# One written list of all steps in place of due times for a list scheduler, in a gated linear attention and gated MLP kernel

## The chip, the cores and the metric

The kernel runs on one core of a Trainium2 chip. The metric is the time of one execution in microseconds (us), measured on the device.

## The reference, cut to what matters

Two parts follow each other: a linear attention with a gated state, and an MLP whose gate mixes the tokens of one batch. There are 4 batches of 768 tokens, 8 heads of 48 features, so 384 features per token.

```
f = 1 / (1 + exp(-f_logit))
for t in range(S):                                   # attention, per batch and head
    state = f[t, :, None] * state + outer(k[t], v[t])
    x[t] = q[t] @ state
h = gelu(x @ w_in)                                   # 384 -> 1024
u, v = h[..., :512], h[..., 512:]
v_n = (v - mean(v)) / sqrt(var(v) + 1e-6) * g_ln
gated = u * (w_sg @ v_n + b_sg)                      # w_sg: 768 x 768 over tokens
out = x + gated @ w_out                              # 512 -> 384
```

`w_in` and `w_out` come as 64-bit words and are converted on the chip.

## The kernel before, in words

The 3072 tokens are 24 tiles of 128, numbered n = 0 to 23, six to a batch; three tiles make a group g = 0 to 7. All work is cut into 1551 named steps: 1533 that the function body adds with `plan.add`, and 18 fillers. A step is nearly always one instruction off TensorE, and a run of matmuls on it. The names that matter here, with the lines that the profile shows:

- Loads on SyncE's queue: `f`, `k`, `q`, `v` of a tile, `cs` (constants: an identity, a triangle, a mask; L1028), `ldin` and `ldout` (two blocks of columns of a weight; L505), `ldsg`, `out`.
- The gate: `e`, `l` (exponential and logarithm on ACT, L435), `cum` (sum over time on TensorE, L632), `up`, `dn` (exponentials on ACT, L435), `mq`, `mk` (q and k times them, L654 and L649).
- The attention of a tile: `tr`, `do` (transposes and decay on TensorE in the first batch, L684 and L669; later batches turn through DRAM instead), `tc`, `di` (copies out, L440), `su` (scores and state update, 64-wide matmuls, L729 and L734), `ms` (mask, L739), `sa`, `sm` (state, L755 and L758), `w` (copy of v, L440), `y` (result, 64-wide matmuls, L777), `ty`, `jy`.
- The MLP: `xT`, `xh`, `xl` (transpose x and split it into two float32r parts), `hv`, `hu` (v and u halves), `gv`, `gu` (GELU on ACT), `ns`, `nd`, `nq`, `nr`, `nh`, `nl` (normalization; `nl` is L867), `sg` (mix over tokens), `sb`, `sm_`, `sh`, `sl` (gate and split), `po` (output matmul), `re` (residual). All large matmuls stand on L801.
- Weights: `wa`, `wp`, `wq`, `wr`, `wc`, `wd`, `we`, `wf` convert a block on ACT, DVE or POOL (L514 to L552); `wT`, `wh`, `wl` do `w_sg`.

Each matmul group takes one of four PSUM buffers (`ps_b`) and gives it back when its reader is done. ACT holds one table at a time: `e`, `l`, `up`, `dn` need one, `gv`, `gu` the other, and each change is an ACT_TABLE_LOAD (L433).

What sets the order: `Plan.run` is a list scheduler with a small model of engine times. `dues` gives each step a due time from its users, `MOVES`, a table of numbers found by search, shifts these and fixes some engines, and the scheduler takes on each engine the ready step with the earliest due time. The result is sorted by the planned start, and each engine's program is that sequence. `Plan.warm` then puts fillers (matmuls of zeros, L1179) on TensorE wherever the plan leaves it idle in the first 45 us: as many columns of 128 as fit the gap by the model. Fillers are real instructions: TensorE runs them whether the gap is there on the chip or not.

Of the kernel before, what the change touches and what calls it, by code (L numbers as in the profile page):

```python
# [71 lines left out]
wpin4:-0.300 wqin4:14.900 wcin4:-0.750 wein4:-3.400:ACT wfin4:21.900 ldin5:7.200 wain5:36.600 wpin5:0.300 wqin5:44.500
wcin5:-0.400 wdin5:17.300 wein5:69.700 ldin6:-164.800 wain6:-41.350 wqin6:23.000 wrin6:24.100 wdin6:-2.500
wein6:-1.400:ACT wfin6:0.000:DVE ldin7:-57.800 wpin7:-0.500 wqin7:-0.100 wrin7:22.500 wdin7:-4.200:DVE wein7:0.600
wfin7:0.000:DVE ldout0:731.600 waout0:-2.000 wqout0:25.950 wrout0:3.950 wcout0:2.100 wdout0:2.900:DVE
weout0:-149.400:ACT wfout0:69.600:POOL ldout1:-12.800 waout1:27.200 wpout1:3.300 wrout1:-7.900 wcout1:-215.200
# [5 lines left out]
f0:-380.900 k0:-176.300 q0:-163.100 v0:-109.900 w0.0:-8.300:DVE w0.1:14.100:ACT cum0:-19.800 up0:-0.800 mq0:4.600
mk0:33.900 do0:1.600 di0:99.700:ACT tc0.0:-101.000:DVE tc0.1:-60.200:ACT ms0:-3.600 sm0.1:-57.100:DVE ty0:0.700
jy0:2.050 xh0:5.000 hv0:17.700 gv0:-3.450 ns0:-11.900 nd0:25.400 nh0:-21.150 nl0:-15.900 re0:-999999918.050
out0:-999999960.000 f1:-357.200 v1:5.350 w1.0:45.900:ACT w1.1:18.500:POOL e1:0.400 l1:32.100 cum1:93.100 up1:100.600
mq1:117.000:POOL mk1:0.000:DVE do1:-20.000 di1:-42.500:ACT tc1.0:48.000:ACT tc1.1:26.300 su1:-7.500 sm1.0:0.800:POOL
sm1.1:61.500 xT1:30.900 xh1:-4.800 xl1:-53.100 hv1:0.600 gv1:6.200 nh1:-6.900 nl1:-126.700 out1:-999999857.100
f2:-115.700 k2:-1.100 q2:16.400 v2:54.000 w2.0:42.300:ACT w2.1:16.000 e2:-65.600 cum2:15.400 up2:-1.400 mq2:0.000:DVE
di2:51.200 tr2:44.700 tc2.0:-0.000:ACT tc2.1:-3.000 su2:-5.700 ms2:26.000 sa2.0:-0.100 sm2.0:-2.100:DVE
sm2.1:58.000:POOL y2:-247.400 ty2:9.450 xT2:0.500 xl2:25.900 ns2:2.400 nd2:42.700 nr2:61.600 nh2:9.000:ACT nl2:11.150  # L90
hu0.0:1148.900 gu0.0:0.800 sb0.0:5.400 sm_0.0:-0.200 sh0.0:-75.200:ACT hu0.1:523.900 gu0.1:77.900 sg0.1:68.000
sb0.1:-21.000 sm_0.1:0.000:DVE hu0.2:51.700 gu0.2:24.200 sg0.2:6.900 sb0.2:-1.350 sm_0.2:15.200:POOL sh0.2:-0.300:ACT
sl0.2:-1.550 hu0.3:-2.300 gu0.3:39.100 sg0.3:5.500 sb0.3:-3.500 sm_0.3:0.000:POOL sh0.3:-230.100:ACT sl0.3:-71.700
po2:17.000 re2:67.300 f3:-2.900 k3:104.100 q3:76.900 v3:55.300 w3.0:0.000:ACT w3.1:18.100:DVE e3:-9.100 l3:-43.700
cum3:-120.000 up3:43.600 dn3:0.100 mq3:2.350:DVE do3:-15.300 di3:-9.200:ACT tr3:22.100 tc3.0:-37.900:ACT
tc3.1:-7.450:ACT su3:138.000 ms3:-197.500 sm3.0:-0.700:DVE sa3.1:-20.250 sm3.1:-0.700 jy3:-1.700 xT3:337.100
xl3:49.600 hv3:14.400 ns3:33.900 nd3:61.000 nq3:25.500 nr3:-15.800 nh3:-7.850 nl3:32.300 po3:6.450 f4:-4.300 q4:26.350
v4:53.000 w4.0:20.150 w4.1:-2.900 e4:40.900 up4:-37.500 dn4:20.000 mq4:1.600:DVE di4:-22.300 tc4.0:0.000:DVE
tc4.1:4.400:DVE ms4:5.900 sa4.0:-20.550 sm4.0:0.000:POOL sm4.1:-20.600:DVE ty4:0.100 jy4:39.150 xT4:27.200 xl4:-0.500
hv4:18.000 ns4:7.500 nq4:37.800 nr4:0.500 nh4:19.400:ACT nl4:53.200 out4:-16.400 f5:-143.700 k5:27.900 q5:33.000  # L100
w5.0:-0.600:DVE w5.1:1.400:POOL e5:157.100 l5:-0.100 cum5:-3.900 dn5:-83.200 mq5:3.700 mk5:1.200:DVE do5:0.900
tc5.0:-9.200 tc5.1:0.500:ACT su5:35.900 sm5.0:-58.600 y5:-65.300 ty5:39.550 jy5:1.400 xl5:7.900 ns5:-27.500
nd5:-44.400:ACT nq5:2.000 nr5:-10.400 nh5:0.000:ACT hu1.0:8.950 gu1.0:-0.050 sg1.0:-54.300 sb1.0:-0.800
sm_1.0:-13.900:POOL sh1.0:121.300 sl1.0:-1.500 hu1.1:-30.500 sg1.1:691.400 sb1.1:0.100 sm_1.1:58.400 sh1.1:15.600:DVE
hu1.2:21.500 sg1.2:-167.000 sm_1.2:8.900:DVE sh1.2:-10.100 sl1.2:-56.500 hu1.3:-34.350 gu1.3:89.000 sm_1.3:7.750:DVE
sl1.3:-0.100 po5:-15.150 re5:-999999877.700 k6:-1.100 v6:1.200 w6.0:-9.400:DVE e6:-2.300 l6:-16.700 lh6:-45.700:DVE
ll6:-23.850:POOL cum6:1679.100 up6:45.550 dn6:-89.650 mq6:-1.900:DVE mk6:-49.900:DVE do6:44.000 tt6.1:2.200
to6:-16.300 ti6.0:50.200 ti6.1:50.000 tc6.0:123.500 tc6.1:13.600:DVE su6:27.700 sz6:-41.350 sa6.0:0.400 sm6.0:-0.800
sa6.1:-0.900 sm6.1:71.700:POOL y6:-3.400 jy6:1.400 xT6:-1.900 xh6:5.300 xl6:-28.900 gv6:-0.500 ns6:2.600 nd6:14.600
nr6:-47.100 nh6:214.400 po6:64.900 out6:-999999809.250 f7:-29.800 k7:6.600 q7:-2.400 v7:-1.100 w7.1:0.000:ACT  # L110
l7:-1.700 lh7:0.000:DVE ll7:-13.500:DVE up7:-1.300 dn7:116.100 mq7:-5.100 mk7:0.000:POOL di7.0:-12.700 tt7.0:12.700
tt7.1:-183.200 ti7.0:22.900 ti7.1:100.050 ti7.2:-0.250 ti7.3:-0.600 tc7.0:108.200:ACT tc7.1:-4.850:DVE sm7.0:0.200
sa7.1:999999923.500 sm7.1:999999864.600 ty7:-0.200 jy7:75.400 xT7:23.000 xh7:-6.800 gv7:119.500 ns7:0.100
nd7:22.200:ACT nr7:3.050 nl7:-3.400 f8:6.000 k8:-51.900 w8.0:-120.600 w8.1:157.900:ACT e8:5.300 l8:-40.200 lh8:-64.200
ll8:-9.100:POOL up8:6.800 mq8:10.800 do8:-34.300 di8.1:9.500 tt8.1:-8.700 ti8.0:-13.300 ti8.1:81.600 ti8.2:153.400
tc8.0:17.300:DVE tc8.1:-10.600:ACT su8:-8.400 ms8:-20.200 sa8.0:999999908.000 sm8.0:59.900:POOL sa8.1:999999905.650
sm8.1:139.700:POOL y8:9.400 ty8:-5.400 xT8:-4.400 xh8:-75.100 xl8:6.600 hv8:-7.800 gv8:0.950 ns8:-129.550 nd8:0.200
nq8:-12.800 nh8:-0.200 nl8:-23.900 gu2.0:2.450 sg2.0:8.000 sb2.0:17.600 sm_2.0:4.700:DVE sh2.0:-78.600 hu2.1:-14.450
sb2.1:5.450 sm_2.1:22.100 sh2.1:71.000 hu2.2:1.000 gu2.2:1.300 sg2.2:11.700 sm_2.2:5.400:POOL sh2.2:0.000:ACT
sl2.2:-18.900 hu2.3:-1.600 gu2.3:-1.800 sg2.3:-2.650 sb2.3:5.400 sm_2.3:0.000:DVE sh2.3:20.100:ACT po8:9.400 re8:4.700  # L120
out8:-999999780.000 f9:0.700 k9:10.600 w9.0:999999899.600 w9.1:-19.400:ACT l9:-30.300 lh9:-10.700:DVE ll9:15.450:POOL
cum9:-472.700 dn9:15.400 mq9:-84.000 mk9:5.500 di9.0:130.900 di9.1:72.600 tt9.0:103.700 ti9.0:-51.200 ti9.1:103.800
ti9.2:-3.500 ti9.3:-30.500 tc9.0:204.500 tc9.1:-12.600 sa9.0:-93.150 sm9.0:-0.400 sa9.1:26.550 sm9.1:64.100 jy9:-0.600
xh9:35.550 xl9:37.200 hv9:-3.100 gv9:153.600 ns9:-11.150 nd9:-4.100:DVE nq9:85.300 nr9:3.000 nh9:0.000:ACT nl9:14.100
po9:22.700 f10:-29.100 q10:0.400 v10:35.200 w10.0:27.600:DVE w10.1:-16.100:POOL e10:94.000 l10:-17.300 lh10:17.600:ACT
# [1173 lines left out]
```

## Time and profile before

| | us |
|---|---|
| median of 3 runs | 364.99 (364.79 to 365.52) |
| the profiled execution, its own time | 364.8 |
| its span, first to last instruction | 363.0 |
| TensorE busy, fillers with it | 355.3 |
| VectorE (DVE) busy | 252.1 |
| ScalarE (ACT) busy | 224.4 |
| GpSimd (POOL) busy | 64.9 |

1.8 us of the execution lie outside the span. The granted clock of TensorE is 1.00 of full speed in all slices of the span. TensorE's busy time counts overlapping matmuls once and takes in the fillers, so it is not all useful work; the idle time of its weight loads (PEld) shows small waits that the busy time hides.

### The profile page before, as it was taken

The page shows a single profiled execution, that of the slowest core. Times are in us where ns is not written, and L with a number is a line of the kernel's source. Part 1 is how long each engine was busy: PE and PEld are TensorE (multiplying, and loading weights), DVE is VectorE, ACT ScalarE, POOL GpSimd, SP SyncE. Part 2 cuts the span into 40 slices and gives each one's busy share as a digit, 9 for nine tenths or more (in the row PEclk, how much of TensorE's full clock was granted, in tenths as well). Part 3 has the DMA queues.
Part 4 walks back from the last instruction along what each step waited for, and adds up shares of the span by engine and source line. Part 5 has one row for each costly group of instructions (what it writes and reads, how often), then busy time and mean ns, then how long its engine had stood idle before and what let it go on. Part 6 is the DMA issues. An engine that isn't in the chain of part 4 may idle for free.

```text
span 363.0 us, 11355 instructions
## 1 busy us (share of the span) xinstructions
PE 355.3 (98%) x4672; PEld 324.1 (89%) x4672; DVE 252.1 (69%) x586; ACT 224.4 (62%) x476; POOL 64.9 (18%) x113
## 2 busy tenths in 40 slices
...
GB/s 195 225 230 198 226 158 251 91 54 161 164 182 205 203 179 223 151 2 117 129 192 135 162 162 118 23 24 109 88 154 70 243 67 2 3 22 2 0 44 94
DMA packets 134047, 45.90 MB, mean 126 GB/s; under 512 B 117221, under 2 KB 130405, under 8 KB 133990
## 3 DMA queue, kind: packets, MB, share of 16 engines
...
## 4 chain that ended last, share of the span: by engine, by line
PE 94%; DMA 3%; ACT 1%; SPq 1%; DVE 0%; issue 0%
PE ps_b L801 69%; PE ps_y L777 7%; PE ps_s L729 4%; PE ps_b L1179 3%; PE ps_b L806 2%; PE ps_s L734 2%; PE ps_b L684 2%; DMA vs<-in_v_dram 1%; PE ps_b L669 1%; DMA cs<-in_consts_dram 1%; PE ps_b L632 1%; PE ps_b L635 1%; PE ps_b L561 1%; PE ps_b L636 1%; PE ps_b L1034 0%; ACT L433 0%
## 5 line engine op out<-in xcount | busy, mean ns | idle before, releaser
L801 PE MATMUL ps_b<-w_sg_hi,vh 128*128 128x384 f32 x192 | 65.5, 341 | 0.0
L801 PE MATMUL ps_b<-w_sg_hi,vh_lo 128*128 128x384 f32 x192 | 64.9, 338 | 0.0
L801 PE MATMUL ps_b<-w_sg_lo,vh 128*128 128x384 f32 x192 | 64.8, 338 | 0.0
L801 PE MATMUL ps_b<-w_out_hi,gg 128*128 128x384 f32 x174 | 48.3, 339 | 0.0
L433 ACT ACT_TABLE_LOAD x29 | 37.2, 1283 | 0.5
L801 PEld LDWEIGHTS ps_b<-w_sg_hi,vh 128*128 128x128 f32 x192 | 36.0, 188 | 0.3
L801 PEld LDWEIGHTS ps_b<-w_sg_lo,vh 128*128 128x128 f32 x192 | 36.1, 188 | 0.0
L801 PEld LDWEIGHTS ps_b<-w_sg_hi,vh_lo 128*128 128x128 f32 x192 | 36.0, 188 | 0.0
L801 PEld LDWEIGHTS ps_b<-w_out_hi,gg 128*128 128x128 f32 x174 | 31.8, 188 | 0.2
L777 PEld LDWEIGHTS ps_y<-vs,st 64*64 64x64 f32 x768 | 24.4, 134 | 5.4 <-issue 3.5
L801 PE MATMUL ps_b<-w_out_lo,gg 128*128 128x384 f32 x87 | 29.1, 335 | 0.0
L801 PE MATMUL ps_b<-xTh,w_in_hi 128*128 128x384 f32 x84 | 29.1, 346 | 0.0
L894 DVE SCALAR_TENSOR_TENSOR tmp<-ps_b,cols,b_bc 128x384 f32<-128x384 f32 x32 | 19.5, 608 | 13.7 <-PE ps_b L801 13.7
L801 PE MATMUL ps_b<-xTl,w_in_hi 128*128 128x384 f32 x84 | 28.4, 338 | 0.0
L801 PE MATMUL ps_b<-xTh,w_in_lo 128*128 128x384 f32 x84 | 28.4, 338 | 0.0
L435 ACT ACTIVATE f<-f 128x384 f32<-128x384 f32 x48 | 25.1, 526 | 4.4 <-DMA f<-in_f_logit_dram 4.0
L777 PE MATMUL ps_y<-vs,st 64*64 64x48 f32 x768 | 27.2, 220 | 0.0
L777 PE MATMUL ps_y<-S,sk 48*64 48x48 f32 x768 | 27.0, 220 | 0.0
L435 ACT ACTIVATE u<-ps_b 128x384 f32<-128x384 f32 x32 | 15.4, 490 | 17.5 <-PE ps_b L801 17.4
L801 PE MATMUL ps_b<-w_in_hi,xTh 128*128 128x512 f32 x63 | 25.6, 406 | 0.4 <-ACT u L435 0.4
L801 PE MATMUL ps_b<-w_in_hi,xTl 128*128 128x512 f32 x63 | 24.9, 395 | 0.0
L801 PE MATMUL ps_b<-w_in_lo,xTh 128*128 128x512 f32 x63 | 24.8, 394 | 0.0
...
## 6 DMA issues: line engine op xcount, KB each, us to landing
...
```

Of the source, the lines that this page charges most:

```text
L433: nc.scalar.preload_act_table_set(SETS[want])
L435: nc.scalar.activation(dst, src, func, **kw)
L561: nc.tensor.transpose(ps[:, j], t[:, (hf * KT + j) * P : (hf * KT + j + 1) * P], ident)
L632: nc.tensor.matmul(ps, tril, f_raw[n], start=True, stop=True)
L684: nc.tensor.transpose(psum[f"tr{n}"][j][:W2, p * P : (p + 1) * P], kq[:, j, 2 * p : 2 * p + 2, :].rearrange("t h d -> t (h d)")[:, :W2], i ...
L729: nc.tensor.matmul(ps_s[rows(score_rows(c, 2 * p + par)), par, p * C : (p + 1) * C], sk[r, 0, p, c], sk[r, 1, p, c], start=True, stop=True)
L734: nc.tensor.matmul(ps_s[feat(par), c, 256 + p * D : 256 + (p + 1) * D], kt[rows(c), h], vs[rows(c), h], start=True, stop=True)
L777: nc.tensor.matmul(ps_y[rows(c), half, h * D : (h + 1) * D], a, m, start=start, stop=stop)
L801: nc.tensor.matmul(ps, a, m, start=(j == 0), stop=(j == len(seq) - 1))
L806: nc.tensor.transpose(ps[:, j], x_sb[n][:, j * P : (j + 1) * P], ident)
L894: nc.vector.scalar_tensor_tensor(t, psum[f"sg{g}.{ft}"][:, :E], g_col[:, ft : ft + 1], b_bc[:, tokens(g)], op0=ALU.mult, op1=ALU.add)
L1179: steps = plan.warm(plan.run(), 45.0, lambda k, n: nc.tensor.matmul(ps_b[k][:, : n * P], zeros, zeros[:, None, :].to_broadcast((P, n, P)), ...
```

## The change

`MOVES`, `dues` and the scheduler's choice go. In their place stands `ORDER`, one list of all 1533 steps, each with its engine where that isn't the step's first choice. `run` walks the list once: each step starts when its engine, its needs, its buffers and its bank are free by the same model, and the steps are again sorted by that start. The functions that issue instructions, the needs, the buffers and `warm` are as before.

```
-MOVES = """
-cs:-176.800 cum_c:-122.400 g:-72.700 b:-1.500 bb0:-18.050 bc0:-65.600:DVE bc1:-30.500 zy:-149.600 zs:1.500
...
+ORDER = """
+clear f0 cs ldin1 k0 ldin4 wain1 e0 l0 f1 q0 f2 ldin6 v0 ldin7 q1 k1 v1 ldin0 k2 f3 cum0 wpin1 wqin1 wrin1 up0 dn0
+wain4 wcin1 wdin1 zs zy wein1 e1 l1 wfin1 wpin4 wqin4 mk0:POOL mq0 tr0 cum1 do0 wain6 tc0.0 tc0.1 up1 di0:ACT dn1
...
     def run(self):
-        self.dues()
-        for name, us, *e in (x.split(":") for x in MOVES.split()):
-            s = self.by[name]
-            s["due"] += float(us)
-            if e:
-                s["engines"] = {e[0]: s["engines"][e[0]]}
...
+        for item in ORDER.split():
+            name, *e = item.split(":")
+            s = self.by[name]
+            e = e[0] if e else next(iter(s["engines"]))
+            s["engines"] = {e: s["engines"][e]}
+            t = max([s["after"], free[e]] + [self.by[x]["end"] + self.SEM for x in s["needs"]])
+            s["got"] = []
             for r in s["take"]:
...
+                at, i = min(self.rings[r])
+                self.rings[r].remove((at, i))
+                s["got"].append(i)
+                t = max(t, at)
```

What the program becomes, in numbers of instructions and steps:

| | before | after |
|---|---|---|
| matmuls other than fillers | the same | the same |
| columns of filler ahead of `cum0` | 1664 | 1920 |
| columns of filler from `cum0` to `y0` | 3072 | 3840 |
| columns of filler after `y0` | 2816 | 896 |
| ACT_TABLE_LOADs of L433 | 29 | 21 |
| the same up to the first `gu` | 5 | 3 |
| steps on ACT, DVE, POOL | 374, 559, 79 | 375, 524, 113 |
| DVE steps ahead of `ns1` (mean of tile 1) | 75 | 62 |
| turns between 64-wide steps (`su`, `y`) and others on TensorE | 58 | 56 |

Of the 13 steps that leave DVE ahead of `ns1`, the balance by kind is `wd` -3, `wf` -3, `w` -3, `mk` -2, `wc`, `wl`, `tc` and `sm` -1 each, `we` +2.

TensorE at the start. The program before, from the first filler to the first `su`; L632 is `cum`, L684 `tr`, L669 `do`:

```order
L1179 MATMUL ps_b_67<-zeros 128x512 x3
L1179 MATMUL ps_b_67<-zeros 128x128
L632 MATMUL ps_b_67<-f,cs 128x384
L632 MATMUL ps_b_68<-f,cs 128x384
L1179 MATMUL ps_b_69<-zeros 128x512
L1179 MATMUL ps_b_67<-zeros 128x512
L1179 MATMUL ps_b_67<-zeros 128x384
L684 MATMUL ps_b_69<-cs,kq_90 112x128 x4
L684 MATMUL ps_b_70<-cs,kq_90 112x128 x4
L669 MATMUL ps_b_67<-cs,eb_102 112x2 x4
```

And now, the same place (L1031 is the filler, L484 `cum`, L536 `tr`, L521 `do`):

```order
L1031 MATMUL ps_b_67<-zeros 128x512 x3
L1031 MATMUL ps_b_67<-zeros 128x384
L484 MATMUL ps_b_67<-f,cs 128x384
L1031 MATMUL ps_b_68<-zeros 128x512 x2
L1031 MATMUL ps_b_67<-zeros 128x512 x3
L1031 MATMUL ps_b_67<-zeros 128x256
L536 MATMUL ps_b_68<-cs,kq_90 112x128 x4
L536 MATMUL ps_b_69<-cs,kq_90 112x128 x4
L484 MATMUL ps_b_70<-f,cs 128x384
L521 MATMUL ps_b_67<-cs,eb_102 112x2 x4
```

Between `cum0` and `tr0` stand 2816 columns of filler where `cum1` and 1408 columns stood; `cum1` comes after `tr0`.

ACT at the start, before; L435 with `flag_e` is `e`, the next `l`, then `up` (`eb`) and `dn`; L514 is `wa`, L440 CAST `we`:

```order
L415 ACT_TABLE_LOAD
L435 ACTIVATE f,flag_e<-f 128x384
L435 ACTIVATE f<-f 128x384
L435 ACTIVATE f,flag_e<-f 128x384
L435 ACTIVATE f<-f 128x384
L514 ACTIVATE u<-gg 128x384
L435 ACTIVATE eb_102<-ps_b_67 128x8x48
L435 ACTIVATE f<-ps_b_67 128x384
```

And now (L287 for L435, L366 for L514):

```order
L267 ACT_TABLE_LOAD
L366 ACTIVATE u<-gg 128x384
L287 ACTIVATE f,flag_e<-f 128x384
L287 ACTIVATE f<-f 128x384
L287 ACTIVATE eb_102<-ps_b_67 128x8x48
L287 ACTIVATE f<-ps_b_67 128x384
L366 ACTIVATE u<-gg 128x384
L292 CAST w_in_hi_75<-u 128x3x128
```

The first `wa` moves ahead of `e0` and `l0`, and `e1`, `l1` move behind `dn0`. On SyncE's queue the loads begin `f0`, `cs`, `ldin1`, `k0`, `ldin4`, `f1`, `q0` where they began `f0`, `f1`, `ldin1`, `cs`, `k0`, `ldin4`, `q0`.

POOL at the start, before, behind the memsets of `clear`; L654 is `mq`, L440 `w`, L758 `sm`, L855 and L856 `nr`:

```order
L1037 MEMSET raw 1x128
L654 ISA
L654 TENSOR_TENSOR kq_91<-kq_91,eb_103 128x8x48
L440 COPY vs_94<-vs_94 64x192
L758 TENSOR_TENSOR S_101<-S_101,dec 112x192
L758 TENSOR_TENSOR S_100<-S_100,dec 112x192
L758 TENSOR_TENSOR S_101<-S_101,dec 112x192
L855 TENSOR_SCALAR vg_rs<-vg_mv 128x1
```

And now (L501 is `mk`, L506 `mq`, L610 `sm`, L388 `wd`, L404 `wf`):

```order
L333 MEMSET cols 128x1
L501 ISA
L501 TENSOR_TENSOR kq_90<-kq_90,f 128x8x48
L506 TENSOR_TENSOR kq_91<-kq_91,eb_103 128x8x48
L966 MEMSET S_100 112x192
L610 TENSOR_TENSOR S_101<-S_101,dec 112x192
L388 TENSOR_TENSOR u<-u 128x384
L610 TENSOR_TENSOR S_101<-S_101,dec 112x192
L404 TENSOR_TENSOR w_in_lo_78<-u,w_in_hi_76 128x3x128 x2
```

`mk0`, `wdin7`, `wfin7` and `wfin5` have come to POOL from DVE, and `mk0` is now its first TENSOR_TENSOR.

## Rows read from the trace of the kernel before

**Rows 1.** The page: busy time of each engine, and the chain of work that ended last by engine.

```profile
PE 355.3 (98%) x4672; PEld 324.1 (89%) x4672; DVE 252.1 (69%) x586; ACT 224.4 (62%) x476; POOL 64.9 (18%) x113
...
PE 94%; DMA 3%; ACT 1%; SPq 1%; DVE 0%; issue 0%
```

**Rows 2.** Busy time of each engine by stretches of the span (us from its start; after the stretch its length, then the engines in the order PE, PEld, DVE, ACT, POOL, TensorE's granted clock, the DMA engines' share, GB/s).

```profile
0.00:20.00 20.00, 17.15 (x186) 10.95 (x187) 13.32 (x33) 12.82 (x31) 2.85 (x14) 1.00 1.03 215
20.00:40.00 20.00, 19.97 (x337) 14.44 (x336) 18.91 (x49) 16.45 (x39) 2.10 (x4) 1.00 0.98 221
40.00:55.00 15.00, 15.00 (x364) 12.24 (x364) 13.13 (x36) 14.71 (x31) 4.80 (x9) 1.00 0.86 174
55.00:70.00 15.00, 14.59 (x146) 12.65 (x139) 11.61 (x30) 14.63 (x36) 3.20 (x6) 1.00 0.66 172
70.00:100.00 30.00, 30.00 (x236) 29.22 (x236) 25.45 (x53) 23.52 (x52) 9.79 (x12) 1.00 0.53 129
```

**Rows 3.** All waits of PE over the span (who, for whom, us in total, times, longest).

```profile
PE ps_b L632 <- DMA cs<-in_consts_dram: 1.8, 1, 1.8
PE ps_b L1179 <- DVE zeros L1181: 1.0, 1, 1.0
PE ps_b L801 <- ACT u L435: 0.4, 1, 0.4
```

**Rows 4.** Waits of the weight loads (PEld) in the first 75 us; the same columns.

```profile
PEld ps_b L801 <- ACT u L435: 0.7, 1, 0.7
PEld ps_b L806 <- ACT sk L440: 0.6, 1, 0.6
```

**Rows 5.** Waits of the weight loads from 75 us to the end, the two longest in total.

```profile
PEld ps_y L777 <- issue: 3.2, 11, 0.4
PEld ps_s L729 <- issue: 1.0, 4, 0.3
```

**Rows 6.** The timeline of the first 16 us, some of its rows: start, us, engine, line, and in brackets the idle time before it and what ended that. L435 `f<-f` is `e` and then `l`, L514 `wa`, L1029 a copy that waits for `cs` alone, L632 `cum`, L1179 the filler, L684 `tr`.

```profile
1.05 4.54 PE L1179 MATMUL ps_b<-zeros 128*128 128x512 f32 x8 [1.05 <-DVE zeros L1181]
...
3.74 0.52 ACT L435 ACTIVATE f<-f 128x384 f32<-128x384 f32 x1 [1.73 <-DMA f<-in_f_logit_dram]
...
4.39 0.52 ACT L435 ACTIVATE f<-f 128x384 f32<-128x384 f32 x1
...
5.19 0.52 ACT L435 ACTIVATE f<-f 128x384 f32<-128x384 f32 x1 [0.28 <-DMA f<-in_f_logit_dram]
...
6.68 0.55 ACT L514 ACTIVATE u<-gg 128x384 f32<-128x384 f32 x1 [0.31 <-DMA gg<-in_moe_w_in_dram]
...
7.28 0.23 DVE L1029 CAST cum<-cs 128x128 fp32r<-128x128 f32 x1 [5.03 <-DMA cs<-in_consts_dram]
...
7.39 1.53 PE L632 MATMUL ps_b<-f,cs 128*128 128x384 f32 x4 [1.80 <-DMA cs<-in_consts_dram]
...
8.76 2.52 PE L1179 MATMUL ps_b<-zeros 128*128 128x512 f32 x6
...
11.12 1.04 PE L684 MATMUL ps_b<-cs,kq 128*112 128x128 f32 x8
```

**Rows 7.** The timeline of TensorE from 18 to 27 us: the first row of `y0`, the filler behind `su1` and the first row of `y1`.

```profile
18.24 0.26 PE L777 MATMUL ps_y<-vs,st 64*64 64x48 f32 x2
...
23.70 2.84 PE L1179 MATMUL ps_b<-zeros 128*128 128x512 f32 x6
26.48 0.26 PE L777 MATMUL ps_y<-vs,st 64*64 64x48 f32 x2
```

**Rows 8.** DVE's groups of the first 40 us: count, busy us, mean ns of one, idle before. L536 is `wd`, L552 `wf`, L649 `mk`, L440 `vs` is `w`, L531 `wc`, L527 (`wr`) the shortest 128x384 operation.

```profile
L531 DVE SCALAR_TENSOR_TENSOR u<-gg,u 128x384 f32<-128x384 uint32 x7 | 4.1, 580 | 0.1
...
L536 DVE TENSOR_TENSOR u<-u 128x384 f32<-128x384 f32 x7 | 3.8, 548 | 0.0
L552 DVE TENSOR_TENSOR w_in_lo<-u,w_in_hi 128x384 fp32r<-128x384 f32 x6 | 3.2, 552 | 0.0
L649 DVE TENSOR_TENSOR kq<-kq,f 128x384 f32<-128x384 f32 x5 | 2.8, 550 | 0.3 <-DMA kq<-in_k_dram 0.3
...
L527 DVE TENSOR_SCALAR u<-u 128x384 uint32<-128x384 uint32 x7 | 2.5, 354 | 0.1
...
L440 DVE COPY vs<-vs 64x192 f32<-64x192 f32 x5 | 1.3, 255 | 0.1
```

**Rows 9.** The page's group of ACT table loads.

```profile
L433 ACT ACT_TABLE_LOAD x29 | 37.2, 1283 | 0.5
```

**Rows 10.** POOL's timeline up to 17 us: its last memset of the start and its first TENSOR_TENSOR.

```profile
2.17 0.20 POOL L1037 MEMSET raw<- 1x128 f32 x1
15.85 1.02 POOL L654 TENSOR_TENSOR kq<-kq,eb 128x384 f32<-128x384 f32 x1 [13.48 <-ACT u L514]
```

**Rows 11.** One DVE line over the span (`nl`): duration in ns min/median/max, first and last start in us.

```profile
L867 DVE SCALAR_TENSOR_TENSOR vh_lo<-vg,vg_rs,vh x24: 707/752/1447, 43.9 to 317.4; 128x512 fp32r<-128x512 f32 x24
```

**Rows 12.** POOL's timeline around 136.5 us, one row.

```profile
136.46 1.01 POOL L649 TENSOR_TENSOR kq<-kq,f 128x384 f32<-128x384 f32 x1 [2.03 <-DVE vg_mv L840]
```

**Rows 13.** DVE's timeline at the same place, the `nl` beside it.

```profile
136.57 1.45 DVE L867 SCALAR_TENSOR_TENSOR vh_lo<-vg,vg_rs,vh 128x512 fp32r<-128x512 f32 x1
```

**Rows 14.** The end: the last residual on DVE.

```profile
358.56 0.56 DVE L925 TENSOR_TENSOR tmp<-ps_b,x 128x384 f32<-128x384 f32 x1 [1.56 <-PE ps_b L801]
```

More of the change, by code (lines that the diff above doesn't have):

```diff
@@ L72 @@
[L72 to L76, printed above, removed]
@@ L82 @@
[L82 to L86, printed above, removed]
@@ L87 @@
[L87 to L125, printed above, removed]
-ll10:84.950 cum10:-17.600 dn10:-12.500 mq10:-6.600:POOL mk10:999999972.750 do10:65.900 di10.0:35.750 di10.1:0.650
```

271 lines of the change are left out of this document (87 added, 184 removed).

## The prediction

> **What bounds the kernel now.** I read the page first, then the stretches, then the waits, then the timeline of the start. TensorE is busy for 355.3 us of the 363.0 us span and carries 94% of the chain that ended last [rows 1]. Over the whole span it waits three times: 1.8 us for `cs`, 1.0 us for the zeros of its own filler, 0.4 us for a GELU [rows 3]. From 75 us on its weight loads show only short waits, most of them "issue" at the 64-wide steps, 0.4 us at most [rows 5]. So nothing done behind the first 75 us can give much: the matmuls are the same in both programs, and there they follow each other without a gap. What is left is the start, where the busy time deceives: it holds 5888 columns of filler behind `cum0`. Those stand where TensorE has nothing to do, because the engines that feed it are late: DVE is busy 18.91 of 20 us from 20 to 40 us, ACT 14.71 of 15 from 40 to 55 and 14.63 of 15 from 55 to 70, while POOL has 2.10 of 20 [rows 2]. The granted clock is 1.00 throughout [rows 2], so a filler column costs the same before and after.
>
> **The change part by part.**
>
> *The first loads and ACT's first steps.* Loads land in the order of the queue. By the first users, `f0` was there at 3.74, `f1` at 5.19, `ldin1` at 6.68, `cs` at 7.28 [rows 6]: steps of 1.45, 1.49 and 0.60 us. `cum0` began at 7.39, 0.11 behind `cs`. Now the queue is `f0`, `cs`, `ldin1`: `cs` at 3.74 + 0.60 = 4.34, `ldin1` at 5.83. So `cs` no longer holds `cum0`; but ACT does the first `wa` ahead of `e0`, so `e0` waits for a weight that it doesn't need. `wa` takes 0.55, `e0` to `l0` 4.39 - 3.74 = 0.65, `l0` 0.52 [rows 6]: 5.83 + 0.55 + 0.65 + 0.52 = 7.55, and with the 0.11 `cum0` begins at 7.66, **0.3 later** than it did. Bounds: 0, if the loads come 0.3 sooner than the steps say; +1.1, if `ldin1` lands no sooner than it did. I take 0.3, the value of the rows themselves. The first filler block ran from 1.05 for 4.54 [rows 6]; 256 columns more, 0.4 by the next paragraph, end it at 6.0, and it is no term.
>
> *Fillers.* Behind `cum0`, 1408 columns ran from 8.76 to the start of `tr0` at 11.12 [rows 6]: 2.36 us, 1.676 ns a column. From `cum0` to `y0` there are now 768 more, +1.3 us; behind `y0` 1920 fewer, -3.2 us. Together 1152 fewer: **-1.9 us**. `y0` itself, at 18.24 before [rows 7], so comes late, at about 18.24 + 0.3 + 1.3 = 19.8, and the gain is made behind it.
>
> *What must hold for that.* TensorE is given its 3.2 us back only if the others feed it sooner after `y0`. For this speaks the work taken from DVE. By the balance of the 13 steps ahead of `ns1`, at 548 ns for `wd`, 552 for `wf`, 550 for `mk`, 580 for `wc`, 255 for `w` [rows 8], -3, -3, -2, -1, -3 make 1.64 + 1.66 + 1.10 + 0.58 + 0.77 = 5.7 us; two `we` come back, which this trace doesn't show on DVE (354 ns is the nearest, the shortest operation of that size [rows 8]): -0.7; `wl`, `tc` and `sm`, one each, are left out as small. So about **5 us of DVE's work** leave a stretch in which it is full, for 3.2 us less filler. On ACT two of five table loads go ahead of the first `gu`, at 1283 ns [rows 9] 2.6 us, in the stretch where it is full. The six table loads that go later are worth nothing: there TensorE waits for nobody [rows 5]. The same holds for the 34 steps that POOL takes over in all, as far as they stand later.
>
> *Old waits.* In 55 to 70 us the weight loads wait 0.7 for a GELU and 0.6 for a copy by ACT [rows 4]; of PE's own time 0.4 is lost [rows 3]. With two table loads fewer ahead of it I take **-0.4** (0 to -1.0).
>
> *Turns.* There are 56 turns between 64-wide and other steps, not 58. No row prices a turn alone; the "issue" waits ahead of 64-wide steps, 3.2 us in 11 [rows 5], are the nearest, 0.3 each and hidden in part: **-0.1** (0 to -0.6).
>
> *New waits.* Fillers absorb lateness; with few left behind `y0`, a late step of ACT, DVE or POOL is now a wait of TensorE. Nearest are the old waits at the places without filler, 0.4 to 0.7 each [rows 3, 4]. One of them: **+0.5** (0 to +3.2, all that was cut there).
>
> *The end* is the same: `po23`, its residual at 358.56 [rows 14], the store. The last gate product goes to POOL, 1.01 [rows 12] for some 0.55, and two output matmul groups stand between it and its reader; no term, and 0.5 if they were not there.
>
> The sum: +0.3 - 1.9 - 0.4 - 0.1 + 0.5 = **-1.6 us**. Against the profiled execution's own 364.8 that gives 363.2; the median of the runs is 0.2 above that execution, so the median after should be **363.4**.
>
> **The rivals.**
>
> *Deeper (chance 0.14).* DVE's 5 us and ACT's 2.6 us are more than the plan spends, so no new wait comes and the old ones go whole: +0.3 - 1.9 - 1.0 - 0.1 = -2.7, a median of 362.3. For it speaks that the filler ahead of `y1`, 2.84 us long [rows 7], stood there while DVE was full; against it, that fillers are run even where the gap is gone, so relief beyond them is worth only the waits.
>
> *POOL holds DVE (0.17).* Where a POOL operation of 1.01 us began at 136.46, an `nl` that began at 136.57 took 1.45 us [rows 12, 13]; the median is 752 ns [rows 11]. So it lost 0.69. Ahead of `su5` POOL now has 14 such steps, not 8. Six times 0.69 is 4.1 us, most of the 5 us that DVE was spared; then three or four waits of 0.4 to 0.7 stand behind `y0`, some 2 us in place of 0.5: 364.9, no change. Against it: only the few that meet lose that much, as the median shows. The Trainium skill has the rule in "SBUF — State Buffer", section "Who interferes with whom": a DVE instruction with two SBUF inputs and a GpSimd one that reads SBUF share a port that one of them holds whole. By that rule a DVE operation that begins just behind a POOL one would lose nearly its whole 1.01, so six of them 6 us as an estimate, and the cut of filler would come back as waits, about 365 too; the trace agrees that the one stands while the other runs, and shows that most don't meet.
>
> *The dense stretch isn't fed (0.11), slower.* Place: TensorE from `y0` to the first `hu`. `su1` now comes straight behind `y0`, and `tr1` ahead of it, so the chains `su`, `sa`, `sm`, `ms`, `y` and `cum`, `up`, `mq`, `tr` must close within about one other step each, on a DVE queue where weight steps stand between. If they take as long as they did, the 3.2 us of filler come back whole as waits, while the 1.3 us ahead of `y0` and the 0.3 of `cum0` stay: +1.5 with the turns, a median of 366.5. It decides from 2.1 us of waits in that stretch, where the sum without new waits (+0.3 - 1.9 - 0.4 - 0.1) is used up. Against it stand the 5 us of DVE's work.
>
> *POOL isn't ready (0.03), slower.* Ahead of its first TENSOR_TENSOR the program has an ISA instruction of POOL; its cost is not in the rows, since 13.48 us of idle time lay over it [rows 10]. Now that first one is `mk0`, which `tr0` needs by about 7.66 + 0.7 + 4.7 = 13.1 (one `cum`, then the filler [rows 6]), so at 1.02 us [rows 10] it must begin by 12.1, 9.7 us behind the memsets. If it needed the whole 13.48 it would begin at 15.9: 3.8 us late, and a median of 367.2. The Trainium skill, "GPSIMD Engine Reference", section "Instruction dispatch", gives about 6 us for the first call of freshly loaded code: by that, ready at 8.4 as an estimate, and no delay. No run here shows it.
>
> **How the numbers follow.** The forecast, 362.8 to 364.2, has 0.55; with the deeper case 0.69 for faster. The case of POOL holding DVE lies within 0.2%, about what a measurement of this kernel can tell from no change (364.3 to 365.7): 0.17. The slower two: 0.14. For the range I go down to the deeper case, 362.2, and up to 365.4, which takes in the larger part of the middle case and leaves out the slower ones and a little at either end, 0.2 in all.
>
> **What would show it.** Right: `cum0` at 7.5 to 7.9; `tr0` at 13 to 13.4 straight behind its filler, not behind a wait; `y0` at 19.5 to 20.2; few PE or weight-load waits between 20 and 55 us; the last residual at 357, not 358.6; DVE below 18 of 20 us from 20 to 40. Wrong: `tr0` released by `mk0` or `mq0` behind the end of its filler (POOL or DVE late at the start); waits of 2.1 us or more between `y0` and the first `hu` (not fed); DVE operations there of twice their median beside POOL's (held); or a wait of TensorE behind 75 us, which would mean that the later order, which I took to be free, costs something.

## The result, and the profile after

| | before | after |
|---|---|---|
| median, us | 365.01 (364.61 to 366.75, 9 executions) | 367.2 (365.98 to 369.7, 9 executions) |
| ratio, 95% interval | | 1.0052 (1.0028 to 1.0076) |
| the profiled execution, its span | 364.8, 363.0 | 369.7, 367.5 |

The kernel became slower by half a per cent; 363.4 had been forecast, with a range up to 365.4. The profiled execution of after is the longest of its nine, so its sizes are near the upper end; a second one is in the first experiment.

The page of after, against [rows 1]:

```profile
PE 356.5 (97%) x4672; PEld 326.4 (89%) x4672; DVE 246.5 (67%) x551; ACT 211.6 (58%) x469; POOL 93.6 (25%) x147
...
PE 76%; DMA 8%; DVE 6%; ACT 4%; SPq 3%; issue 2%; POOL 0%; ACTq 0%; DVEq 0%
```

TensorE's share of the chain fell from 94% to 76%, and DMA, DVE and SyncE's queue are in it: a first sign that TensorE is no longer fed without a gap. The stretches, columns as in [rows 2]:

```profile
0.00:20.00 20.00, 17.76 (x120) 10.17 (x120) 12.34 (x26) 11.75 (x27) 4.74 (x15) 1.00 1.07 215
20.00:40.00 20.00, 19.57 (x400) 16.21 (x399) 17.78 (x40) 15.72 (x38) 6.39 (x8) 0.91 1.04 214
40.00:55.00 15.00, 15.00 (x366) 12.71 (x365) 13.09 (x35) 13.61 (x33) 4.49 (x9) 1.00 0.48 119
...
70.00:100.00 30.00, 29.70 (x234) 29.11 (x233) 25.41 (x52) 22.59 (x48) 11.90 (x13) 1.00 0.68 153
```

DVE is relieved (17.78 of 20 us from 20 to 40, forecast below 18), but not by the 5 us of work that the prediction counted: ahead of `ns1` its busy time is 30.0 us in place of 31.2, with 13 steps fewer. New against this profile of before is the granted clock, 0.91 in that stretch: it stands at 0.50 of full speed (1.2 GHz) for 3.4 us from 32.3. The timeline of TensorE there (L536 is `tr3`, L484 `cum5`):

```profile
32.33 1.89 PE L536 MATMUL ps_b<-cs,kq 128*112 128x128 f32 x8
34.01 1.06 PE L1031 MATMUL ps_b<-zeros 128*128 128x256 f32 x2
34.87 1.25 PE L484 MATMUL ps_b<-f,cs 128*128 128x384 f32 x2
```

The same eight transposes took 1.04 at full speed [rows 6]. All waits of PE, against [rows 3]:

```profile
PE ps_s L581 <- DVE sk L292: 2.0, 1, 2.0
PE ps_b L484 <- ACT f L287: 1.2, 1, 1.2
PE ps_b L1031 <- DVE zeros L1033: 1.0, 1, 1.0
PE ps_y L629 <- ACT vh_lo L703: 0.6, 1, 0.6
PE ps_b L658 <- DVE x L637: 0.4, 2, 0.3
PE ps_b L653 <- DVE tmp L746: 0.3, 1, 0.3
PE ps_b L653 <- DVE vg_mv L692: 0.3, 1, 0.3
```

The first, fourth, sixth and seventh lie behind 77 us, where the kernel before had none. Laying the program's order against the rows gives where TensorE's steps began:

| us | `cum0` | `tr0` | `y0` | first `hu` | first `sg` | `hold`, TensorE's last | end of the span |
|---|---|---|---|---|---|---|---|
| before | 7.39 | 11.12 | 18.24 | 55.26 | 77.98 | 358.45 | 363.0 |
| after | 7.69 | 13.16 | 20.14 | 55.18 | 77.43 | 362.26 | 367.5 |

Up to the first `sg` after is 0.55 ahead; from there to `hold` it takes 284.83 in place of 280.47 (+4.4), from `hold` to the end 5.2 in place of 4.6 (+0.65), and 2.2 in place of 1.8 lie outside the span: -0.55 + 4.4 + 0.65 + 0.4 = +4.9, all of the 369.7 - 364.8. Of the 4.4 the waits of PE behind 77 us make 3.2; the rest stands in no line of that table. Three of these waits, in order.

**Ahead of the second `sg` step (82 us).** DVE's timeline, then POOL's:

```profile
80.17 1.18 DVE L292 COPY vs<-vs 64x192 f32<-64x192 f32 x1
81.38 0.62 DVE L746 SCALAR_TENSOR_TENSOR tmp<-ps_b,cols,b_bc 128x384 f32<-128x384 f32 x1
...
80.01 0.34 POOL L292 COPY vs<-vs 64x192 f32<-64x192 f32 x1
80.29 0.95 POOL L895 MEMSET raw<- 128x1024 f32 x1
```

The copy `w6.1` takes 1.18 where such a copy took 0.255 [rows 8], and ends 0.1 behind POOL's memset; `sb0.0` behind it (L746) then releases the bank that TensorE waits for.

**Ahead of `y11` (143 us).** DVE's timeline, then SyncE's queue; L610 is `sm11.0`, L591 `ms11`:

```profile
141.52 0.36 DVE L610 TENSOR_TENSOR S<-S,dec 112x192 f32<-112x192 f32 x1 [1.21 <-DMA dec<-dec_d]
141.79 0.42 DVE L292 COPY sk<-raw 112x512 f32<-112x512 f32 x1
142.13 0.48 DVE L696 TENSOR_SCALAR vg<-vg,vg_mv 128x512 f32<-128x512 f32 x1
142.53 0.68 DVE L591 TENSOR_TENSOR st<-ps_s,cs 128x512 f32<-128x512 f32 x1
...
132.90 1.78 SPq L446 DMA_DIRECT2D kq<-in_q_dram  x1
...
138.35 0.95 SPq L513 DMA_DIRECT2D dec<-dec_d  x1
```

DVE stands for 1.21 us for a load of 48x8 numbers, which the new list has put behind `k13`, `q13` and five other loads on SyncE. `ms11`, which needs nothing of that load, is queued behind. The table of waits names ACT's `vh_lo` for TensorE's 0.6 us; that had long been done, and `y11` began at 143.36, 0.15 behind `ms11`.

**Ahead of `su16` (203 us).** TensorE, DVE, POOL, SyncE:

```profile
203.06 0.34 PE L581 MATMUL ps_s<-sk 48*64 48x64 f32 x8 [1.96 <-DVE sk L292]
...
200.25 2.76 DVE L292 COPY sk<-raw 112x512 f32<-112x512 f32 x2 [1.52 <-DMA raw<-kq_d]
...
200.12 1.01 POOL L506 TENSOR_TENSOR kq<-kq,eb 128x384 f32<-128x384 f32 x1
201.09 0.69 POOL L610 TENSOR_TENSOR S<-S,dec 112x192 f32<-112x192 f32 x1
201.74 0.99 POOL L751 TENSOR_TENSOR tmp<-tmp,u 128x384 f32<-128x384 f32 x1
...
194.00 0.59 SPq L446 DMA_DIRECT2D kq<-in_q_dram  x1
194.63 2.46 SPq L561 DMA_DIRECT2D raw<-kq_d  x1
```

The fourth piece of tile 16 (`ti16.3`) stands behind `k18` and `q18`; its issue alone took 2.46 us. Then the two copies took 2.76 us beside three POOL operations.

### The profile page after: what moved, and what is told of

Read it like the earlier page. It is cut to its first block, busy times and chain, and to the rows that moved or that the text cites. A ratio compares the mean times of both kernels' runs of the same rounds, so it can differ in the third digit from the quotient of the medians.

```text
span 367.5 us, 11345 instructions
## 1 busy us (share of the span) xinstructions
PE 356.5 (97%) x4672; PEld 326.4 (89%) x4672; DVE 246.5 (67%) x551; ACT 211.6 (58%) x469; POOL 93.6 (25%) x147
## 4 chain that ended last, share of the span: by engine, by line
PE 76%; DMA 8%; DVE 6%; ACT 4%; SPq 3%; issue 2%; POOL 0%; ACTq 0%; DVEq 0%
PE ps_b L653 57%; DMA raw<-kq_d 5%; PE ps_y L629 4%; PE ps_s L581 3%; PE ps_b L1031 2%; PE ps_b L658 2%; PE ps_s L586 2%; PE ps_b L536 2%; SPq L561 1%; DMA out_dram<-tmp 1%; ACT sk L292 1%; DMA gg<-in_moe_w_in_dram 1%; DVE sk L292 1%; PE ps_b L413 1%; PE ps_b L484 1%
## 5 line engine op out<-in xcount | busy, mean ns | idle before, releaser
L751 POOL TENSOR_TENSOR tmp<-tmp,u 128x384 f32<-128x384 f32 x20 | 21.3, 1069 | 69.0 <-DVE tmp L746 66.8
L610 POOL TENSOR_TENSOR S<-S,dec 112x192 f32<-112x192 f32 x25 | 16.9, 675 | 54.8 <-DVE S L607 40.2
L746 DVE SCALAR_TENSOR_TENSOR tmp<-ps_b,cols,b_bc 128x384 f32<-128x384 f32 x32 | 19.3, 607 | 16.7 <-PE ps_b L653 16.6
L292 ACT CAST gg<-tmp 128x384 fp32r<-128x384 f32 x18 | 8.9, 512 | 34.7 <-POOL tmp L751 32.4
L581 PE MATMUL ps_s<-sk 48*64 48x64 f32 x768 | 23.7, 229 | 2.1 <-DVE sk L292 2.0
```

The source lines that it names most:

```text
L292: (nc.scalar.copy if e == "ACT" else ENG[e].tensor_copy)(dst, src)
L581: nc.tensor.matmul(ps_s[rows(score_rows(c, 2 * p + par)), par, p * C : (p + 1) * C], sk[r, 0, p, c], sk[r, 1, p, c], start=True, stop=True)
L610: ENG[e].tensor_mul(state_to(n, c), state_to(n, c), decay(n, c))
L746: nc.vector.scalar_tensor_tensor(t, psum[f"sg{g}.{ft}"][:, :E], g_col[:, ft : ft + 1], b_bc[:, tokens(g)], op0=ALU.mult, op1=ALU.add)
L751: ENG[e].tensor_mul(t, t, uT.pop((g, ft)))
```

## The experiments

"The list" is that of the change; line numbers differ between kernels. Unless said otherwise only the list differs.

**The list again**, with no edit.

> The list of the change once more, on the same chip as the three mixed lists. Theory L (the loss is made behind sg0.0, at some 77 us, by late loads and by DVE standing while POOL runs): 366.3 to 367.5, with a TensorE wait of 1 to 2 us somewhere behind 75 us, not necessarily at the same place. Theory S (the loss is made in the start, where fillers are few and the granted clock fell for 3.4 us): the same time, with the clock at 1.2 GHz again near 32 us and small waits behind 75 us.

Measured: 366.54 (365.29 to 369.32), ratio 1.0044 (1.0021 to 1.0067). The pattern is the same: first `sg` at 77.80, from there to `hold` 283.24, to the end 5.21; the clock fell again, from 32.0 to 35.4. Its waits behind 77 us:

```profile
PE ps_y L673 <- DVE st L635: 0.9, 1, 0.9
PE ps_s L625 <- DVE sk L336: 0.6, 1, 0.6
...
PE ps_b L697 <- DVE tmp L790: 0.3, 1, 0.3
```

So the three places are the same in both profiles and their sizes vary: `y11` 0.6 to 0.9, `su16` 0.6 to 2.0.

**Either half alone**, cut at the first `sg` of TensorE:

```diff
+e1 = change[:change.index("sg0.0")];  e1 += [s for s in before if s not in e1]
+e2 = before[:before.index("sg0.0")];  e2 += [s for s in change if s not in e2]
```

> The list of the change up to sg0.0, from there the order and the engines of the kernel before. Theory L: the start is worth what was forecast or half of it and the rest is as before, 363.3 to 364.5, sg0.0 at 76 to 77.5 us, no TensorE wait over 0.6 us behind it. Theory S: the loss stays, 366 to 367.

> The order and engines of the kernel before up to sg0.0, from there the list of the change. Theory L: the loss comes without the gain of the start, 367 to 368.5, sg0.0 at 78 us as before and waits of TensorE behind it. Theory S: 365 as before, or a little better by the two turns.

Measured: the new start with the old rest 365.15, ratio 1.0001 (0.9983 to 1.0018); the old start with the new rest 368.06, 1.0066 (1.0042 to 1.0091). In the first the first `sg` came at 76.05, 1.9 ahead of before and with the clock at 1.00, and 1.5 went at the seam, where TensorE waits once for a GELU; what was left of the lead was gone at 118 us. So the start with the order of before behind it isn't worth the 363.3 to 364.5 of Theory L either. In the second the first `sg` came at 79.97 (the clock fell, at 46 us) and from there to `hold` it took 282.97, 2.5 more than before. The loss lies behind the first `sg`.

**POOL's later steps taken back**: 50 steps behind the first `sg` (16 `sm_`, 12 `sm`, 11 `w`, 9 `mk` and `mq`, 2 `ll`), 47 to DVE and three of the copies `w` to ACT, where they had been; a few of them:

```diff
-w7.1:POOL sm_0.0:POOL mk8:POOL mq9:POOL sm7.0:POOL
+w7.1:ACT sm_0.0:DVE mk8:DVE mq9:DVE sm7.0:DVE
```

> The list of the change, with the 50 steps behind sg0.0 that it gave to POOL and that were on DVE before back on DVE, at the same place of the list. If POOL's hold on DVE makes the later waits: 364 to 365.3. If late loads make them: 366 to 367.5, about as the change. If the DVE steps are needed on POOL, since DVE is full there: over 367.5.

Measured: 367.91, ratio 1.0072 (1.0048 to 1.0095); from the first `sg` to `hold` 284.96. DVE's copies of `sk` behind 77 us, in before, in after and in this kernel:

```profile
L440 DVE COPY sk<-raw 112x512 f32<-112x512 f32 x14 | 5.8, 423 | 4.0 <-DMA raw<-kq_d 1.9 <-PE ps_y L777 1.1 <-issue 0.9
```
```profile
L292 DVE COPY sk<-raw 112x512 f32<-112x512 f32 x12 | 7.9, 662 | 3.2 <-DMA raw<-kq_d 3.2
```
```profile
L335 DVE COPY sk<-raw 112x512 f32<-112x512 f32 x12 | 4.9, 418 | 0.6 <-DMA raw<-kq_d 0.6
```

A copy lasts 418 ns again, but DVE has 47 steps more to do, and TensorE waits at other places. POOL's part lengthens DVE's work; taking it away is no cure.

**Two loads moved** (SyncE's steps of the list alone), and then the copy behind `sb0.0` as well:

```diff
-v12 k13 q13 di12.1 ti12.3 ti12.2 ti12.0 ti12.1 di11.0
+v12 di11.0 k13 q13 di12.1 ti12.3 ti12.2 ti12.0 ti12.1
-ti16.1 ti16.2 ti16.0 di16.1 k18 q18 ti16.3
+ti16.1 ti16.2 ti16.0 di16.1 ti16.3 k18 q18
```
```diff
-w6.1 sb0.0
+sb0.0 w6.1
```

> The list of the change with two small loads moved on SyncE's queue: di11.0 (a decay of tile 11) stands ahead of the loads k13 and q13 and not behind them, and ti16.3 (one of four turned pieces of tile 16) ahead of k18 and q18. Nothing else differs. Theory Loads: in the change sm11.0 waits on DVE for that decay (1.2 to 1.5 us) and holds ms11, so that TensorE waits ahead of y11 (0.8 to 1.1 us); and both copies of tile 16 wait on DVE for ti16.3, so that TensorE waits ahead of su16 (0.7 to 2.1 us). With the loads earlier both waits go: 1.5 to 2.2 us less than the 366.5 to 367.2 of the change, 364.5 to 365.2. Rival Full DVE: the loads are only the last of several late things, DVE's queue is late there anyhow, the same waits come back with another cause: 366.2 to 367.

> As the run before, and on DVE the copy w6.1 stands behind sb0.0 and not ahead of it. In the change that copy of 64x192 took 1.18 us in place of 0.26 beside POOL's zr, sb0.0 began 0.6 late and TensorE waited 0.5 us for it ahead of sg0.2. Theory Port (a copy that meets POOL's operation holds what is queued behind it): that wait goes too, 0.3 to 0.6 below the run before, 364.0 to 364.8. Rival: sb0.0 meets the same POOL operation in the copy's place, no difference from the run before.

Measured: 365.91 (363.7 to 367.87), ratio 1.0009 (0.9989 to 1.0029), and 366.12 (364.32 to 366.95), 1.0003 (0.9985 to 1.002). In the first DVE does `sm11.0` at 140.63 with no wait ahead of it, and the two copies of tile 16 in 0.76 and not 2.76; both waits of TensorE are gone:

```profile
140.63 0.35 DVE L654 TENSOR_TENSOR S<-S,dec 112x192 f32<-112x192 f32 x1
...
199.80 0.76 DVE L336 COPY sk<-raw 112x512 f32<-112x512 f32 x2
```

In ratio the loads are worth 0.0035, some 1.3 us; in the median 0.6 to 1.3, less than expected; in this execution three smaller waits came in their place (0.6 for `x` at 141 us, 0.3 for `xTl` at 152, 0.5 for a GELU at 154.5). It is the longest of its twelve, and from the first `sg` to `hold` it takes 283.29, no less than the list again. Over several profiles the gain shows, if not in this one: 281.1 to 283.3 in the four with the loads moved (this and three below), 282.7 to 284.8 in the six with the list's later steps as they were, 280.47 before. So 0.6 to 2.8 us remain there that no run takes apart. What the copy adds can't be told from nothing in the medians; in the profile the wait ahead of the second `sg` is gone.

**512 columns of filler**, where TensorE waits anyway (0.17 us at 30.5 in after), on the list; and then with the loads and the copy:

```diff
             last = s["start"] + s["engines"]["PE"] + 0.05
+            n = dict(do3=2, xT1=2).get(s["name"], 0)
+            if n:
+                more.append(dict(name="warm", on="PE", bank=0, fn=lambda e, k=s["at"][0], n=n: fn(k, n)))
             more.append(s)
```

> The list of the change with 512 columns of filler more: 256 ahead of do3 and 256 ahead of xT1 (28 to 31 us), where TensorE waits 0.2 to 0.4 us anyway. Theory Clock: in two of two profiles of the change the granted clock fell to 0.5 of full speed (1.2 GHz) for 3.41 us from 32 us, behind transposes, two decays of 2 columns and 64-wide steps, and cost 1.4 to 1.6 us at cum5; with the filler it stays at 1.00, the first sg of the first batch begins at 76 to 76.6 and not at 77.4 to 77.8, and the median is 0.8 to 1.3 below the change, 365.3 to 366.2. Rival No cure: the fall comes anyway, at another place, and the filler costs 0.3 to 0.6: 366.8 to 367.5.

> All three edits together: the two loads, the copy w6.1 and the filler. If the three causes (loads, port, clock) are the loss and add up: 366.6 to 367.2 less 1.8, less 0.5, less 1.1, so 363.2 to 363.8, below the kernel before (365.0) and close to the time that was forecast for the change. If only the loads count: 364.5 to 365.4. If none of them: 366.5 to 367.5.

Measured: 366.68 (365.85 to 369.71), ratio 1.004 (1.002 to 1.006); with the others 365.6 (364.91 to 367.64), 1.0013 (0.9996 to 1.0031). The clock is 1.00 in the stretch in which it fell (filler alone):

```profile
30.00:35.00 5.00, 5.00 (x94) 4.33 (x92) 3.52 (x9) 3.24 (x10) 1.48 (x2) 1.00 1.05 297
```

The median did not follow: the filler costs about what the falls cost on average. That these 512 columns hold the clock the counts show. A fall can be read from an execution's mean granted clock: the six profiles with one ahead of `hold` have 0.991 to 0.994, the eleven without 0.996 to 1.000. Over the experiments with the list's start as it is, 23 of 80 executions have 0.995 or less; of those with the 512 columns 2 of 60. Of the kernel before, with its longer fillers, it is 21 of 106 (366.4 us, the others 365.0): the falls are not new, and that the change makes them more frequent isn't shown. Nor are they the loss: in the list as it is the executions without a fall, 16 of 21, have a median of 366.5.

**DVE's program as long as before**:

```diff
         nc.vector.memset(zeros, 0.0)
+        for _ in range(21):
+            nc.vector.memset(padding, 0.0)
```

> The list of the change as it is, with 21 memsets of one element more on DVE at the very start, where DVE waits for the first loads; so DVE's program has as many instructions as that of the kernel before (716 in the trace against 695). Theory End: in the change DVE's next instruction behind its branch at the end begins 3.4 us after it (before: 0.6), so that the execution ends 5.2 us behind the start of the last TensorE step and not 4.6, and 2.1 us lie outside the span and not 1.8; how long it takes goes with the length of DVE's program and not with the order. With the padding the end takes 4.2 to 4.7 us, and the median is 0.5 to 1.0 below the change, 365.7 to 366.4. Rival: the end depends on the order of the last steps, the padding does nothing, 5.2 us, 366.5 to 367.2.

> Everything together: the two loads, the copy w6.1, the 512 columns of filler and the 21 memsets on the list of the change. If the end is a part of its own: 0.5 to 1.0 below the run with the first three (365.6), 364.6 to 365.1, no slower than the kernel before. If not: 365.4 to 365.9.

Measured: 366.62 (365.7 to 367.98, 6 executions), ratio 1.0052 (1.0036 to 1.0069), the time that the rival gave; with everything 364.95 (363.66 to 366.23), 0.9997 (0.998 to 1.0014). But in the two profiles the end takes 4.6 and 4.7 us, as the theory said. The last residual, then the span, of the padded list:

```profile
359.16 0.56 DVE L822 TENSOR_TENSOR tmp<-ps_b,x 128x384 f32<-128x384 f32 x1 [1.56 <-PE ps_b L698]
...
span 363.6 us, 11366 instructions
```

and of after:

```profile
362.37 0.56 DVE L777 TENSOR_TENSOR tmp<-ps_b,x 128x384 f32<-128x384 f32 x1 [1.56 <-PE ps_b L653]
...
span 367.5 us, 11345 instructions
```

4.5 us against 5.1. Behind that residual DVE has a branch: by the records of its instructions the next one begins 3.35 us after the branch in after, and 0.6 us after it before. In every profile with 695 to 700 instructions of DVE the end took 5.2 to 5.3 us, in every one with 715 to 742 it took 4.2 to 4.7, whatever the order of the last steps. The Trainium skill, "Runtime: NRT & Kernel Launch", section "Instruction fetch mechanics", says that a taken branch whose target isn't in the pages held forces a fetch before the engine goes on; the 3.35 us against 0.6 agree with that, though the records don't show which fetch DVE stood for. The 0.3 us outside the span stayed with the padding (2.1). They go with the length of GpSimd's program: the nine kernels with 238 instructions of POOL in the trace have 2.0 to 2.15 outside (medians), the eight with 148 to 228 have 1.8 to 1.9; no run changed that alone, and why it is so I did not find. For the padded list alone the median shows no gain in six executions; for the sum of all it is 0.65 (365.6 to 364.95), within the two intervals.

With everything mended, the list's profile shows no wait of PE behind 25 us:

```profile
PE ps_b L532 <- ACT f L335: 1.3, 1, 1.3
PE ps_b L1079 <- DVE padding L1083: 1.1, 1, 1.1
PE ps_b L706 <- DVE x L685: 0.3, 1, 0.3
PE ps_b L584 <- DVE kq L549: 0.2, 1, 0.2
```

**The list up to 84 us, or up to 235 us**, and from there the order of before, with `w6.1` behind `sb0.0`:

```diff
+e10 = change[:change.index("su6")];    e10 += [s for s in before if s not in e10]
+e11 = change[:change.index("sg5.0")];  e11 += [s for s in before if s not in e11]
```

> The list of the change up to su6 (84 us), with w6.1 behind sb0.0, and from there the order and the engines of the kernel before. Theory Behind (the start gains what was forecast, the loss is made behind it): sg0.0 at 76.0 to 76.5, no wait at sg0.2, the end in 4.2 to 4.6 us, the median 363.4 to 364.4, below both kernels. Rival Trade (the relief of the first 75 us is paid for with work that is only put off, so that the order of before can't be fed behind it): waits of 1 us or more between 84 and 130 us, 365 to 366.

> As the run before, but the list of the change up to sg5.0 (235 us), and the order of before from there. Theory Behind: the waits ahead of y11 and su16 are back, 1.5 to 3 us, so 1.5 to 2.5 us above the run before, 365.3 to 366.3. Rival Last third (the loss is made behind 235 us): no more than 0.5 above the run before.

Measured: 364.7 (363.55 to 366.64), ratio 0.9987 (0.9964 to 1.0009), and 367.06 (366.34 to 367.52), 1.0051 (1.0036 to 1.0066). The second is 2.4 us longer: the waits ahead of `y11` and `su16` are back (0.8 and 0.6), and the end took 5.25 (DVE has 700 instructions). In the first the first `sg` came at 76.03. Its twelve executions fall in two groups: four with a mean granted clock of 0.994 took 365.9 to 366.6, eight with 0.997 or more 363.6 to 365.2, median 364.1.

Even so the start's lead isn't handed on. It is 1.95 us at the first `sg`, 1.7 at `su6` (88.64 against 90.33), 1.2 behind a wait of 0.3 for DVE's `ll` at 104.9, and 0.35 at the `sg` behind a GELU (117.74 against 118.09), where TensorE waits 0.6. ACT stands ahead of that GELU for a load that came 0.2 sooner than before; this kernel, then before:

```profile
113.06 1.14 ACT L336 COPY sk<-raw 112x512 f32<-112x512 f32 x2 [2.71 <-DMA raw<-kq_d]
...
117.00 0.60 ACT L331 ACTIVATE vg<-ps_b 128x512 f32<-128x512 f32 x1
```
```profile
113.27 1.15 ACT L440 COPY sk<-raw 112x512 f32<-112x512 f32 x2 [1.81 <-DMA raw<-kq_d]
...
117.21 0.60 ACT L435 ACTIVATE vg<-ps_b 128x512 f32<-128x512 f32 x1
```

Before, TensorE waited for nobody there, but only just: the GELU ended 0.3 us ahead of that `sg`.

**The first weight behind `e0` and `l0`**, on the list; then the list up to 84 us with the filler, without and with this:

```diff
-ldin4 wain1 e0 l0 f1
+ldin4 e0 l0 wain1 f1
```

> The list of the change with the first wa behind e0 and l0 on ACT and not ahead of them; nothing else is moved, but the fillers follow the plan: 1024 columns ahead of cum0 and not 1920, and 3840 between cum0 and tr0 and not 2816. Theory First (the weight that ACT does first costs the start what cum0 is late: 7.6 to 8.7 us in the profiles of the change's start, against 7.39 in the kernel before): cum0 at 5 to 6, tr0 0.3 to 0.8 earlier, the median 0.3 to 0.8 below the change, 365.8 to 366.6. Rival Chain: tr0 waits for mq0, whose DVE queue hangs on the same weight, so tr0 comes no earlier: 366.4 to 367.2.

> The list of the change up to su6 (84 us) with w6.1 behind sb0.0 and the 512 columns of filler ahead of do3 and xT1, and from there the order of the kernel before. Without the filler this gave 364.7, in which executions with a mean granted clock of 0.994 took 365.9 to 366.6 and those of 0.997 and more 363.6 to 365.2. Theory Clock: with the filler such executions become rare, the median is 363.9 to 364.4, below both kernels by more than 0.2%. Rival: the falls have another cause, they come as often, and the filler costs 0.3: 364.7 to 365.3.

> As the run before, with e0 and l0 ahead of the first wa. Theory First: another 0.3 to 0.8 less, 363.3 to 364.0. Rival Chain: no difference from the run before, 0.2 either way.

Measured: 368.59 (366.51 to 368.94, 6 executions), ratio 1.0078 (1.0048 to 1.0107); 364.67 (363.97 to 365.56), 0.9978 (0.9962 to 0.9994); 364.69 (364.22 to 365.71), 0.9988 (0.9972 to 1.0005). With `e0` first `cum0` came at 4.80, 2.9 earlier, and `tr0` at 12.15, 1.0 earlier, but `y0` at 20.31, no earlier, and the clock was low in five of six executions, which the Chain theory did not foresee. The second is the best kernel here, 0.4 us below before: the clock holds in all twelve executions, yet the median is that of the same list without the filler, near the time that its rival gave (364.7), though the falls did go. No kernel reached the 363.4 of the forecast.

## Why the prediction was wrong, point by point

**The step that failed** is the sentence that what lies behind 75 us can't give much, and the use made of it: that the six later table loads and the later steps of POOL are worth nothing, so that the later order has no term at all. That TensorE didn't wait there showed only that there was nothing to win. In the list there are three waits at the same places in both profiles; from the first `sg` to `hold` it takes 2.2 to 4.4 us more than before in six profiles. The halves and the cut at 84 us show the place, the moved loads the cause of the two largest waits, worth some 1.3 us: small loads behind large ones on SyncE's queue, a DVE step that waits for one, and behind it the step that TensorE needs. The rest of the 2.2 to 4.4 stays open. I had compared SyncE's sequence only for the first loads. The same step failed a second time: a lead won in the start counted as won at the end. With the order of before behind it, the lead of 1.95 us was 0.35 at 118 us, where a load and a GELU behind it come when they came before.

**The end**, for which I took no term, cost 0.65 in the span; the padding gave it back in the profile. It hung on the number of DVE's instructions, which the table in the change showed as DVE's 524 steps against 559.

**Fillers**, -1.9: right up to the first `sg` where the clock held. In the five profiles with the list's start as it is and no fall of the clock the first `sg` came at 76.0 to 77.3, 0.7 to 1.95 ahead of before; the dense stretch was fed. The reason given for it was right by luck: DVE was spared 1.2 us ahead of `ns1`, not 5, and TensorE was fed all the same. Wrong is that the clock is 1.00 throughout: it falls in three of ten executions of this start, at some 2 us each (366.15 against 364.1 in the cut at 84), and in two of ten of before, at 1.4. Keeping 512 columns stopped the falls and cost as much.

**The first loads**, +0.3: `cum0` at 7.69 against 7.66, but 7.6 to 8.7 over the profiles, past the upper bound of +1.1, and worth little: with `cum0` 2.9 earlier `y0` came no sooner. `tr0` (13.16) and `y0` (20.14) came as forecast in this profile; in the eight others of this start they came at 13.1 to 14.2 and 20.4 to 21.1, later than the 20.2 given. **Old waits**: the GELU's 0.4 at 64 us is gone. **New waits**, +0.5: right up to 75 us (0.4 for `x`), wrong as the whole. **Turns**: not told apart.

**The rivals.** *Not fed* gives 366.5, near the result by chance: between `y0` and the first `hu` TensorE waited 0.4 us, not 2.1. *POOL holds DVE* came true for DVE at its place and nearly at its size, and yet not for TensorE. Between 16 and 39 us four operations of DVE beside POOL's take 1.25 to 1.53 us, 3.6 in all above the medians of their lines (4.1 had been put on six); before has none such there. One of them, DVE and then POOL, where [rows 8] have 354 ns:

```profile
37.23 1.53 DVE L379 TENSOR_SCALAR u<-u 128x384 uint32<-128x384 uint32 x1
...
36.90 0.66 POOL L610 TENSOR_TENSOR S<-S,dec 112x192 f32<-112x192 f32 x1 [2.97 <-DVE S L607]
37.52 1.03 POOL L501 TENSOR_TENSOR kq<-kq,f 128x384 f32<-128x384 f32 x1
```

So the 5 us less that DVE had to do became 1.2; the wait of TensorE that was to follow didn't come (0.4 us between `y0` and the first `hu`). Where POOL's hold did cost TensorE is later, at `w6.1` and at the copies of tile 16. In both, DVE's copy ends 0.1 to 0.3 us behind the last of POOL's operations beside it. The Trainium skill, "SBUF — State Buffer", section "Who interferes with whom", counts copies among the DVE operations that can take the port shared with GpSimd, and has the second comer wait for the whole of the other's operation; these rows agree, and the copy waits there for more than one operation of POOL in a row. *POOL isn't ready*: `mk0` was done 2.6 us ahead of `tr0`. *Deeper* fell with the forecast.

Still open: what makes the rest of the loss behind the first `sg`, the 0.3 us outside the span, and why the filler that holds the clock costs as much as it saves.
